# Local value products in four matmuls, earlier in the step, with head split and evacuation reordered

## The chip, the cores and the metric

One core of a Trainium2 chip runs the whole kernel. The metric is device time in microseconds (us) of one execution, here the median of three runs. The engines are TensorE (PE, matmuls; its weight loads are listed apart as PEld), VectorE (DVE), ScalarE (ACT), GpSimd (POOL, almost unused) and SyncE (SP, which issues the DMAs). Each engine runs its own queue of instructions; semaphores tie them together. [...]

## What is computed

```python
# attention: 8 batches x 8 heads, 512 local and 32 global positions, head size 64
k_all = concat([k_g, k_l]);  v_all = concat([v_g, v_l])
out_g = sm(scale * q_g @ k_all.T) @ v_all            # global rows see everything
s_ll  = where(abs(pos[:, None] - pos[None, :]) <= 32, scale * q_l @ k_l.T, -1e9)
s_lg  = scale * q_l @ k_g.T
out_l = sm(concat([s_lg, s_ll])) @ concat([v_g, v_l])   # local rows: a band and the 32 global keys
attn  = concat([out_g, out_l])
# MLP on 4608 tokens of width 512, hidden width 2048
x   = attn.transpose(0, 2, 1, 3).reshape(-1, 512)
h   = maximum(x @ w_in, 0)
out = (h * h) @ w_out
```

## The kernel before

The work is one loop over steps t (from line 593), and three stages run in it side by side. Each step takes one "head", a half sequence (256 rows) of one batch and head; there are 128 of them (NT). In step t the scores and the softmax belong to head t, the transposes and value products to head t-1, and the MLP to step m = t - 9, which is an eighth of the hidden width for a block of 256 rows. So 128 head steps and 136 MLP steps overlap in most of the loop.

Precision is kept by splitting: a value is rounded to a matmul type (`hi`, `ph`, `x_h`, `gh`: the head) and the rounding error is kept in a second tensor (`lo`, `pl`, `x_l`, `gl`: the rest). A product of two split tensors is then three matmuls: head by head, head by rest and rest by head. Heads are made by ACT copies, rests by DVE subtractions. The first 16 heads (`plain`, t < 16) skip this. "Late" below means steps t from 17 to 128, in which head t-1 is not plain.

A late step issues, in this order (line 598 on; each engine keeps its own part of this order, as `InOrder` asks from t = 17):

- `transposes(t-1)`: four PE transposes of the probabilities into the PSUM tile `pt`; `scores(t)`: four matmuls into `s`.
- `gemm1(m, 0)`: 12 matmuls of 256 columns, the first half of the first MLP product, into `h`.
- `pt_split(t-1)`: four ACT copies make the heads `ph` (128x256, 64x128, twice 32x256).
- `softmax1(t)`: DVE, two masked maxima (the profile's CUSTOM_DVE_ANT_0) and their scaling; `softmax2(t)`: ACT, two exponentials. `pt_rest(t-1)`: DVE, three subtractions, into `pl` and the lower half of `ph`.
- Jobs of the global rows at "place 3", and every eighth step `evac` (ACT copies an output block and SP stores it).
- `gemm1(m, 1)`: 12 matmuls. `av(t-1)`: nine value products into the PSUM tile `xa`. `g_scores(t)`: one matmul into `gs`.
- `softmax3(t)`: DVE, sum plus epsilon, reciprocal, and the scaling of both halves of the probabilities.
- `act1(m)`: ACT relu of `h`, then the square, on ACT where t modulo 16 is in `SQ` (2, 3, 4, 5, 14, 15), else a DVE product.
- `x_evac(t-1)`: ACT copies `xa` to `x_h`, DVE subtracts into `x_l`. `split_head(t+1)`: one ACT copy of 864 columns into `hi`, three DVE rests (`lo` 128x448, then parts of `hi`, 64x352 and 32x64).
- `g_evac` in odd steps; jobs at "place 2"; `gemm2(m-1, 0)` and `gemm2(m-1, 1)`: 12 matmuls of 512 columns into `o`; `act2(m)`: ACT copy `gh`, DVE rest `gl`; jobs at "place 1".

The global rows need extra jobs, two groups of heads in 16 steps (line 652). With t modulo 16 they are: `g_soft` (a DVE maximum) in 12 and 2; `g_norm` (DVE) in 13 and 3, and at the end of these steps `g_tr` (four PE transposes into `gt`); `g_rest` and `g_split_v` (ACT and DVE) in 14 and 4, with `g_av` (13 PE matmuls into `gxo`) at the end; `g_x` (four DVE transposes) in 15 and 5 and again in 2 and 8; a second `g_split_v` in 0 and 6, at place 2, and a second `g_av` at the end of 1 and 7.

[...] 

```python
xa = ps_a.tile([64, HALF], F32, tag="xa", name=f"xa{t}")     # av
gt = ps_a.tile([P, 512], F32, tag="xa", name=f"gt{t}")       # g_tr
xo = ps_a.tile([64, P], F32, tag="xa", name=f"gxo{t}_{pair}")  # g_av
```

[...]

Of the kernel before, what the change touches and what calls it, by code (L numbers as in the profile page):

```python
# [7 lines left out]
F32 = mybir.dt.float32  # L8
F32R = mybir.dt.float32r
# [7 lines left out]
P = 128  # L17
HALF = 256
NGR = 2 * B
NT = NGR * H  # L20
QC, KC, VC = HALF, 352, 256
PK = QC + KC + VC
# [4 lines left out]
LAG = 9  # L27
NPLAIN = 16
# [1 line left out]
PLAN = [",,,b", "b,,,b", "b,,,b", "b,,b,", "b,,b,", "b,,b,", "b,,b,", "b,b,,b", "b,b,,b", "bb,bb,bb,bb", "bb,bb,bb,bb", "bbs,bb,bbs,bbs", "bbs,bbs,bbs,bbs", "bbs,bbs,bbs,bbs", "bbs,bbs,bs,s", "ss,s,s,s", "ss,s,s,s", "s,,s,", "s,,s,", "s,,s,", "s,,s,", "s,,s,", "s,,s,"]  # L30
FREE = (17, 17, 17)
LOOK = 2
SQ = (2, 3, 4, 5, 14, 15)
MUL = 9
WCH = 32

# [1 line left out]
def f(ap):  # L38
    return ap.bitcast(F32)
# [19 lines left out]
def attention_moe(  # L59
# [22 lines left out]
    def plain(t):  # L82
        return t < NPLAIN
# [3 lines left out]
    def w_take(n):  # L87
        w_bufs["free"] -= n
# [36 lines left out]
    def split_head(t):  # L125

        hd = heads[t]
        raw = hd["raw"]
        if plain(t):
            return  # L130
        hi = p2.tile([P, PK], F32R, tag="hi", name=f"hi{t}")
        lo = p2.tile([P, QC + 192], F32R, tag="lo", name=f"lo{t}")
        ac.copy(hi, raw)
        ve.tensor_sub(lo, raw[:, KC : KC + QC + 192], f(hi[:, KC : KC + QC + 192]))
        ve.tensor_sub(hi[64:, :KC], raw[64:, :KC], f(hi[64:, :KC]))
        ve.tensor_sub(hi[32:64, PK - 64 :], raw[32:64, PK - 64 :], f(hi[32:64, PK - 64 :]))
        hd["hi"], hd["lo"] = hi, lo

    def scores(t):
# [45 lines left out]
    def softmax3(t):  # L185
        st = heads[t]["st"]
        pr = prob[t % 2]
        ve.tensor_scalar(out=st[:, 6:8], in0=st[:, 4:6], scalar1=1e-9, scalar2=None, op0=ALU.add)
        ve.reciprocal(out=st[:, 0:2], in_=st[:, 6:8])
        for u in range(2):  # L190
            w_ = pr[:, WIN * u : WIN * (u + 1)]
            if MUL <= t < NPLAIN:
                ac.activation(out=w_, in_=w_, func=AF.Copy, scale=st[:, u : u + 1])
            else:
                ve.tensor_scalar(out=w_, in0=w_, scalar1=st[:, u : u + 1], scalar2=None, op0=ALU.mult)
# [6 lines left out]
    def pt_split(t):  # L202
        hd = heads[t]
        if plain(t):
            pts = p2.tile([P, 512], F32, tag="gh", name=f"pts{t}")
            ac.copy(pts, pt)
            hd["pts"] = pts
            return
        ph = p1.tile([P, 640], F32R, tag="ph", name=f"ph{t}")
        pl = p1.tile([P, 256], F32R, tag="pl", name=f"pl{t}")  # L210
        ac.copy(ph[:, :256], pt[:, :256])
        ac.copy(ph[:64, 256:384], pt[:64, 320:448])
        for r in (0, 32):
            ac.copy(ph[r : r + 32, 384:640], pt[64:96, 256:512])
        hd["ph"], hd["pl"] = ph, pl

    def pt_rest(t):
        if plain(t):
            return
        ph, pl = heads[t]["ph"], heads[t]["pl"]  # L220
        ve.tensor_sub(pl, pt[:, :256], f(ph[:, :256]))
        ve.tensor_sub(ph[64:, 256:384], pt[:64, 320:448], f(ph[:64, 256:384]))

        ve.tensor_sub(ph[64:, 384:640], pt[64:, 256:512], f(ph[:64, 384:640]))

    def av(t):
        hd = heads[t]
        c = QC + KC
        if plain(t):

            xa = ps_a.tile([P, HALF], F32, tag="xa", name=f"xa{t}")
            v, pts = hd["raw"][:, c:], hd["pts"]
            mm = [
                (xa, v[:, 0:128], pts[:, 256:512]),
                (xa[:, 0:128], v[:, 64:192], pts[:, 0:128]),
                (xa[:, 128:256], v[:, 128:256], pts[:, 128:256]),
            ]
        else:
            xa = ps_a.tile([64, HALF], F32, tag="xa", name=f"xa{t}")
            vh, vl, ph, pl = hd["hi"][:, c:], hd["lo"][:, QC:], hd["ph"], hd["pl"]  # L240
            mm = []
            for u in range(2):
                o, vs, ps = xa[:, 128 * u : 128 * u + 128], slice(64 * u, 64 * u + 64), slice(128 * u, 128 * u + 128)
                mm += [(o, vh[:, vs], ph[:, ps]), (o, vl[:, vs], ph[:, ps]), (o, vh[:, vs], pl[:, ps])]
            o = xa[:, 64:192]
            mm += [(o, vh[:, 128:192], ph[:, 256:384]), (o, vl[:, 128:192], ph[:, 256:384])]
            mm.append((xa, vh[:, 192:256], ph[:, 384:640]))
        for i, (o, a, b) in enumerate(mm):
            pe.matmul(o, a, b, start=i == 0, stop=i == len(mm) - 1, skip_group_check=True)
        hd["xa"] = xa[:64, :]  # L250

    def x_evac(t):
        g, h = divmod(t, 8)
        xa = heads[t]["xa"]
        r = slice((h % 2) * 64, (h % 2) * 64 + 64)
        if g == 0:
            ac.copy(xg[r, h // 2, :], xa)
        else:
            ac.copy(x_h[r, g % 2, h // 2, :], xa)
            ve.tensor_sub(x_l[r, g % 2, h // 2, :], xa, f(x_h[r, g % 2, h // 2, :]))  # L260
        heads[t] = None

    state = {}
# [176 lines left out]

    moe = {}

    def gemm1(m, j):
        blk, st = divmod(m, 8)
        if j == 0:
            moe["hp"] = ps_h.tile([P, 2, HALF], F32, tag="h", name=f"h{m}")
        hp = moe["hp"]
        if blk == 0:
            mm = [(win(wf, st, j, c), xg[:, c, :]) for c in range(4)]
        else:  # L450
            xh, xl = x_h[:, blk % 2], x_l[:, blk % 2]
            mm = []
            for c in range(4):
                wh, wl = win(whi, st, j, c), win(wlo, st, j, c)
                mm += [(wh, xh[:, c, :]), (wh, xl[:, c, :]), (wl, xh[:, c, :])]
        for n, (a, b) in enumerate(mm):
            pe.matmul(hp[:, j, :], a, b, start=n == 0, stop=n == len(mm) - 1)

    def act1(m):
        hp = moe["hp"]  # L460
        pool, tag = (p2, "gl") if m < 8 else (p1, "r")
        r = pool.tile([P, 2, HALF], F32, tag=tag, name=f"r{m}")
        ac.activation(out=r, in_=hp, func=AF.Relu)
        if m < 8 or m + LAG < NT + 8 and (m + LAG) % 16 in SQ:
            ac.activation(out=r, in_=r, func=AF.Square)
        else:
            ve.tensor_mul(r, hp, r)
        moe["r"] = r
# [33 lines left out]

    def evac(blk, tiles=(0, 1)):
        for i in tiles:
            pool, tag = ((p1, "ot"), (p2, "gl"))[i]
            ot = pool.tile([P, DM], F32, tag=tag, name=f"ot{blk}_{i}")
            ac.copy(ot, moe["o"][i])
            if blk < NGR:
# [80 lines left out]
    for t in range(NSTEP + LAG + 1):  # L589
# [31 lines left out]
        w_tick(t, 0)  # L621
        if live and early:
            g_scores(t)
        if run:
            gemm1(m, 1)
        if prev:
            av(t - 1)
        if live and not early:
            g_scores(t)
        if early and t + 1 < NPLAIN:  # L630
            scores(t + 1)
        if live and not early:
            softmax3(t)
        if run:
            act1(m)
        if prev:
            x_evac(t - 1)
            if plain(t - 1):
                w_take(-1)
        if early:  # L640
            softmax3(t)
        w_tick(t, 1)
        if t + 1 < NT:
            split_head(t + 1)
        if live:
            if t % 2 == 1:
# [124 lines left out]
```

## Time and profile before

| | |
|---|---|
| median of 3 runs | 1068.78 us (1068.65 to 1068.86) |
| the profiled execution | 1068.82 us, its span 1067.0 us |
| PE busy | 1050.4 us, 98% |
| DVE busy | 856.3 us, 80% |
| ACT busy | 753.1 us, 71% |
| DMA | 96.78 MB, mean 91 GB/s |

The span runs from the first to the last profiled instruction; the execution's own time has some 1.8 us more around it. Nearly every instruction is issued through the helper at line 52, so lines do not tell groups apart; the tile names do. A group reads "output<-inputs", then sizes as partitions x elements. A row of the timeline has start, length, engine, line, operation, tiles, shape and count, and in brackets the idle time before it with what ended it. PE rows overlap, because matmuls are pipelined: the distance of two starts is the price of one, not its length.

### The profile page before, as it was taken

To read this page: it belongs to the slowest core of one execution; us is meant where nothing else is said; L and a number is where in the kernel's file an instruction comes from. 1 tells how busy PE (TensorE), PEld (TensorE's weight loads), DVE (VectorE), ACT (ScalarE), POOL (GpSimd) and SP (SyncE) were. 2 spreads that over 40 slices of the span, in tenths; PEclk is the share of its full clock that TensorE was granted. 3 is DMA by queue.
4 is the path that set the end of the run, shared out by engine and by line. 5 is a ranking of instruction groups with operands and counts; after the bars stand their busy time and mean duration, and the time that the engine had idled before them with its cause. 6 is when DMAs were issued, how large, how long until landed. Compare 5 with 4: busy or idle time off the path is not lost.

```text
span 1067.0 us, 21142 instructions
## 1 busy us (share of the span) xinstructions
PE 1050.4 (98%) x7568; PEld 941.7 (88%) x7568; DVE 856.3 (80%) x2687; ACT 753.1 (71%) x1901; POOL 3.9 (0%) x14
## 2 busy tenths in 40 slices
PE   7999999999999999999999999999999999999998
PEld 6776889999998989998999989999999989999896
DVE  5698988898888989988888888888888888874321
ACT  5898877778777776778777777777777787774322
POOL 1000000000000000000000000000000000000000
PEclk9999999999999999999999999999999999999999
DMA  9772132223222322222322222223221322201000
GB/s 372 310 263 74 57 106 76 71 80 98 68 89 64 103 65 83 74 91 77 94 71 82 86 72 76 90 66 100 78 89 55 94 86 66 88 29 33 13 20 20
DMA packets 54312, 96.78 MB, mean 91 GB/s; under 512 B 4288, under 2 KB 29376, under 8 KB 54208
## 3 DMA queue, kind: packets, MB, share of 16 engines
q1 hardware_dynamic: 54064, 95.37, 27.2%
q8 instruction: 60, 0.98, 0.4%
q14 instruction: 44, 0.36, 0.1%
q10 hardware_dynamic: 144, 0.07, 0.0%
HBM read 86.51 MB, written 8.91 MB: 89 GB/s over the span
## 4 chain that ended last, share of the span: by engine, by line
PE 87%; ACT 7%; DVE 4%; issue 1%; DMA 0%; ACTq 0%
PE o L52 33%; PE h L52 32%; PE xa L52 7%; PE s L52 6%; PE pt L52 5%; PE gxo L52 2%; PE gs L52 2%; ACT prob L52 1%; DVE prob L52 1%; ACT r L52 1%; ACT ph L52 1%; ACT hi L52 1%; ACT ot L52 1%; PE gt L52 1%; ACT sg L52 0%
## 5 line engine op out<-in xcount | busy, mean ns | idle before, releaser
L52 PE MATMUL h<-x_h,ws 128*128 128x256 f32 x2048 | 388.9, 283 | 0.0
L52 PEld LDWEIGHTS h<-x_h,ws 128*128 128x128 f32 x2048 | 327.0, 191 | 0.5
L52 PE MATMUL o<-ws,gh 128*128 128x512 f32 x1024 | 321.3, 395 | 0.0
L52 PE MATMUL h<-x_l,ws 128*128 128x256 f32 x1024 | 289.1, 282 | 0.1
L52 PEld LDWEIGHTS o<-ws,gh 128*128 128x128 f32 x1024 | 185.5, 188 | 34.6
L52 PE MATMUL o<-ws,gl 128*128 128x512 f32 x512 | 202.6, 396 | 0.0
L52 PEld LDWEIGHTS h<-x_l,ws 128*128 128x128 f32 x1024 | 195.9, 191 | 0.9 <-DVE x_l L52 0.4
L52 ACT CAST ph<-pt 128x256 fp32r<-128x256 f32 x448 | 141.1, 341 | 67.7 <-PE pt L52 60.8
L52 ACT ACTIVATE prob<-prob,st 128x224 f32<-128x224 f32 x270 | 127.8, 475 | 61.2 <-DVE st L52 59.1
L52 ACT ACTIVATE r<-h 128x512 f32<-128x512 f32 x136 | 81.4, 599 | 112.3 <-PE h L52 112.3
L52 PEld LDWEIGHTS o<-ws,gl 128*128 128x128 f32 x512 | 96.2, 188 | 22.7
L52 DVE CUSTOM_DVE_ANT_0 prob<-s,con 128x224 f32<-128x224 f32 x256 | 90.0, 386 | 24.5 <-PE s L52 23.2
L52 DVE TENSOR_TENSOR gl<-r,gh 128x512 fp32r<-128x512 f32 x128 | 87.9, 686 | 23.3 <-ACT gh L52 20.5
L52 ACT CAST hi<-raw 128x864 fp32r<-128x864 f32 x112 | 102.5, 915 | 1.4
L52 DVE TENSOR_TENSOR r<-h,r 128x512 f32<-128x512 f32 x82 | 56.7, 692 | 51.9 <-ACT r L52 50.6
L52 PE MATMUL xa<-ph,hi 128*64 128x128 f32 x448 | 87.3, 238 | 1.6 <-DVE ph L52 1.2
L52 DVE TENSOR_TENSOR hi<-raw,hi 64x352 fp32r<-64x352 f32 x224 | 82.5, 368 | 6.4
L52 ACT CAST gh<-r 128x512 fp32r<-128x512 f32 x128 | 79.1, 618 | 9.1 <-DVE r L52 8.7
L52 DVE TENSOR_TENSOR ph<-pt,ph 64x128 fp32r<-64x128 f32 x224 | 79.6, 355 | 7.0
L52 DVE TENSOR_TENSOR lo<-raw,hi 128x448 fp32r<-128x448 f32 x112 | 69.6, 622 | 15.3 <-ACT hi L52 12.5
L52 PE MATMUL pt<-con,prob 128*128 128x128 f32 (+1 forms) x512 | 78.2, 274 | 0.7 <-ACT prob L52 0.5
L52 DVE TENSOR_SCALAR prob<-prob,st 128x224 f32<-128x224 f32 x242 | 70.7, 334 | 4.1
(80 smaller groups left out, 1572.7 us busy)
## 6 DMA issues: line engine op xcount, KB each, us to landing
raw<-in_pk_dram SPq DMA_DIRECT2D x127, 432.0 KB, 3.2
wr<-in_w_dram SPq DMA_DIRECT2D x32, 512.0 KB, 7.9
gv<-in_vg_dram SPq DMA_DIRECT2D x32, 320.0 KB, 3.3
out_dram<-ot SPq DMA_DIRECT2D x32, 256.0 KB, 2.2
qr<-in_qg_dram SPq DMA_DIRECT2D x31, 64.0 KB, 2.8
out_dram<-ot SPq DMA_DIRECT2D x8, 64.0 KB, 1.7
con<-in_consts_dram SPq DMA_DIRECT2D x2, 224.0 KB, 5.1
raw<-in_pk_dram SPq DMA_DIRECT2D x1, 304.0 KB, 3.2
```

The source lines that it names most:

```text
L52: r = method(*args, **kwargs)
```

## The change

- The split copy of a head holds value heads and value rests side by side (`vs`, 4 blocks of 64 + 64 columns); the head data differ in one duplicated block that is left out. One ACT copy of 608 columns and one of 4 x 64 replace the one of 864; the DVE rests are 128x256, 64x352 and 128x256.
- The heads and rests of the transposed probabilities lie side by side in one tile `ps`; three ACT copies instead of four, three DVE rests as before.
- `av` has four matmuls (one of 128 columns, three of 256) into `xa`, which is now 128 partitions by 512 columns: rests times heads and heads times rests land in separate parts.
- `x_evac` adds these parts: one ACT copy, then three DVE operations of 64x256 with a new tile `xr`, instead of one.
- `av` stands after the first six matmuls of `gemm1(m, 1)`, not after all twelve.
- The order after `softmax3` is `split_head(t+1)`, `x_evac(t-1)`, `act1(m)`; it was `act1`, `x_evac`, `split_head`.
- In `softmax3`, the scaling of the second half of the probabilities is on ACT; all squares up to t = 127 are on ACT, later ones on DVE.
- The first output tile of `evac` is staged in the buffer of tag "pth" instead of "ot".

```diff
-SQ = (2, 3, 4, 5, 14, 15)
...
+        c = QC + KC
+        hi = p2.tile([P, c + 2 * VC + QC], F32R, tag="hi", name=f"hi{t}")
+        lo = hi[:, c + 2 * VC :]
+        vr = raw[:, c:].rearrange("p (b n) -> p b n", b=4)
+        vs = hi[:, c : c + 2 * VC].rearrange("p (b n) -> p b n", b=4)
+        ac.copy(hi[:, :c], raw[:, :c])
+        ac.copy(vs[:, :, :64], vr)
+        ve.tensor_sub(lo, raw[:, KC:c], f(hi[:, KC:c]))
         ve.tensor_sub(hi[64:, :KC], raw[64:, :KC], f(hi[64:, :KC]))
+        ve.tensor_sub(vs[:, :, 64:], vr, f(vs[:, :, :64]))
...
-            if MUL <= t < NPLAIN:
+            if MUL <= t < NPLAIN or t >= NPLAIN and u == 1:
                 ac.activation(out=w_, in_=w_, func=AF.Copy, scale=st[:, u : u + 1])
...
+        ps = p1.tile([P, 896], F32R, tag="ph", name=f"ph{t}")
+        pb = ps[:, :512].rearrange("p (u h n) -> p u h n", u=2, h=2)
+        ac.copy(pb[:, :, 0, :], pt[:, :256].rearrange("p (u n) -> p u n", u=2))
+        ac.copy(ps[:64, 512:640], pt[:64, 320:448])
+        ac.copy(ps[:64, 640:], pt[64:, 256:])
...
+        ve.tensor_sub(pb[:, :, 1, :], pt[:, :256].rearrange("p (u n) -> p u n", u=2), f(pb[:, :, 0, :]))
+        ve.tensor_sub(ps[64:, 512:640], pt[:64, 320:448], f(ps[:64, 512:640]))
+        ve.tensor_sub(ps[64:, 640:], pt[64:, 256:], f(ps[:64, 640:]))
...
+            xa = ps_a.tile([P, 512], F32, tag="xa", name=f"xa{t}")
+            xb = xa.rearrange("p (u h n) -> p u h n", u=2, h=2)
+            ps, vs = hd["ps"], [hd["hi"][:, c + 128 * i : c + 128 * i + 128] for i in range(4)]
+            both = bass.AP(xa.tensor, xa.offset + 64, [list(xa.ap[0]), [192, 2], [1, 64]])
+            mm = [(both, vs[2], ps[:, 512:640]), (xb[:, :, 0, :], vs[3], ps[:, 640:])]
+            mm += [(xa[:, 256 * u : 256 * u + 256], vs[u], ps[:, 256 * u : 256 * u + 256]) for u in range(2)]
...
+            ac.copy(x0, xb[:64, :, 0, :])
+            ve.tensor_sub(xr, xb[:64, :, 0, :], f(x0))
+            ve.tensor_add(xr, xb[:64, :, 1, :], xr)
+            ve.tensor_add(x1, xb[64:, :, 0, :], xr)
...
-            pe.matmul(hp[:, j, :], a, b, start=n == 0, stop=n == len(mm) - 1)
+            if half in (None, 2 * n // len(mm)):
+                pe.matmul(hp[:, j, :], a, b, start=n == 0, stop=n == len(mm) - 1)
...
-        if m < 8 or m + LAG < NT + 8 and (m + LAG) % 16 in SQ:
+        if m + LAG < NT:
             ac.activation(out=r, in_=r, func=AF.Square)
...
-            pool, tag = ((p1, "ot"), (p2, "gl"))[i]
+            pool, tag = ((p1, "pth"), (p2, "gl"))[i]
...
+        late = prev and not plain(t - 1)
         if run:
-            gemm1(m, 1)
+            gemm1(m, 1, 0 if late else None)
         if prev:
             av(t - 1)
+        if run and late:
+            gemm1(m, 1, 1)
...
         if live and not early:
             softmax3(t)
+        if late:
+            if t + 1 < NT:
+                split_head(t + 1)
+            x_evac(t - 1)
         if run:
             act1(m)
-        if prev:
+        if prev and not late:
             x_evac(t - 1)
```

More of the change, by code (lines that the diff above doesn't have):

```diff
@@ L130, in split_head @@
             return
[L131 to L134, printed above, removed]
+        c = QC + KC
[6 more added lines that the diff above has]
+        ve.tensor_sub(lo, raw[:, KC:c], f(hi[:, KC:c]))
         ve.tensor_sub(hi[64:, :KC], raw[64:, :KC], f(hi[64:, :KC]))
-        ve.tensor_sub(hi[32:64, PK - 64 :], raw[32:64, PK - 64 :], f(hi[32:64, PK - 64 :]))
+        ve.tensor_sub(vs[:, :, 64:], vr, f(vs[:, :, :64]))
         hd["hi"], hd["lo"] = hi, lo
@@ L208, in pt_split @@
             return
[L209 to L215, printed above, removed]
+        ps = p1.tile([P, 896], F32R, tag="ph", name=f"ph{t}")
[3 more added lines that the diff above has]
+        ac.copy(ps[:64, 640:], pt[64:, 256:])
+        hd["ps"], hd["pb"] = ps, pb
     def pt_rest(t):
@@ L219, in pt_rest @@
             return
[L220 to L224, printed above, removed]
+        ps, pb = heads[t]["ps"], heads[t]["pb"]
+        ve.tensor_sub(pb[:, :, 1, :], pt[:, :256].rearrange("p (u n) -> p u n", u=2), f(pb[:, :, 0, :]))
+        ve.tensor_sub(ps[64:, 512:640], pt[:64, 320:448], f(ps[:64, 512:640]))
+        ve.tensor_sub(ps[64:, 640:], pt[64:, 256:], f(ps[:64, 640:]))
     def av(t):
@@ L238, in av @@
         else:
[L239 to L247, printed above, removed]
+            xa = ps_a.tile([P, 512], F32, tag="xa", name=f"xa{t}")
[4 more added lines that the diff above has]
+            mm += [(xa[:, 256 * u : 256 * u + 256], vs[u], ps[:, 256 * u : 256 * u + 256]) for u in range(2)]
         for i, (o, a, b) in enumerate(mm):
             pe.matmul(o, a, b, start=i == 0, stop=i == len(mm) - 1, skip_group_check=True)
-        hd["xa"] = xa[:64, :]
+        hd["xa"] = xa
     def x_evac(t):
@@ L256, in x_evac @@
         if g == 0:
-            ac.copy(xg[r, h // 2, :], xa)
-        else:
-            ac.copy(x_h[r, g % 2, h // 2, :], xa)
-            ve.tensor_sub(x_l[r, g % 2, h // 2, :], xa, f(x_h[r, g % 2, h // 2, :]))
+            ac.copy(xg[r, h // 2, :], xa[:64, :])
+            heads[t] = None
+            return
+        x0, x1 = x_h[r, g % 2, h // 2, :], x_l[r, g % 2, h // 2, :]
+        if plain(t):
+            ac.copy(x0, xa[:64, :])
+            ve.tensor_sub(x1, xa[:64, :], f(x0))
+        else:
+            xb = xa.rearrange("p (u h n) -> p u h n", u=2, h=2)
+            x0, x1 = [x.rearrange("p (u n) -> p u n", u=2) for x in (x0, x1)]
+            xr = p1.tile([P, 2, P], F32, tag="xr", name=f"xr{t}")[r]
+            ac.copy(x0, xb[:64, :, 0, :])
+            ve.tensor_sub(xr, xb[:64, :, 0, :], f(x0))
+            ve.tensor_add(xr, xb[:64, :, 1, :], xr)
+            ve.tensor_add(x1, xb[64:, :, 0, :], xr)
         heads[t] = None
@@ L441, in attention_moe, with gemm1 @@
     moe = {}
-    def gemm1(m, j):
+    def gemm1(m, j, half=None):
         blk, st = divmod(m, 8)
@@ L633, in attention_moe @@
             softmax3(t)
+        if late:
+            if t + 1 < NT:
+                split_head(t + 1)
+            x_evac(t - 1)
         if run:
             act1(m)
-        if prev:
+        if prev and not late:
             x_evac(t - 1)
-            if plain(t - 1):
-                w_take(-1)
+            w_take(-1)
         if early:
@@ L642, in attention_moe @@
         w_tick(t, 1)
-        if t + 1 < NT:
+        if t + 1 < NT and not late:
             split_head(t + 1)
@@ L729 @@
             pk[:, hf, :, 64 * dup : 64 * dup + 64, c + 128 : c + 192] = vw[:, :, 128:192]
-        for dup in range(3):
-            pk[:, hf, :, 32 * dup : 32 * dup + 32, c + 192 : c + 256] = v_g
+        for dup in range(2):
+            pk[:, hf, :, 64 * dup : 64 * dup + 32, c + 192 : c + 256] = v_g
     pk = pk.reshape(NT, P, PK)
```

## The prediction

> **What bounds the kernel now.** I read the page first, then the windows, the chain that ended last, and the timeline of VectorE (DVE), ScalarE (ACT) and TensorE (PE) over single steps; a step is one pass of the main loop. The page says that PE is busy for nearly the whole span.
>
> ```profile
> span 1067.0 us, 21142 instructions
> PE 1050.4 (98%) x7568; PEld 941.7 (88%) x7568; DVE 856.3 (80%) x2687; ACT 753.1 (71%) x1901; POOL 3.9 (0%) x14
> ```
>
> In the steps that the change touches, DVE is nearly as full. The windows give for 150 us: PE 149.63 busy, then PEld, DVE 130.91, ACT 110.59, and a granted clock of 1.00.
>
> ```profile
> 550.00:700.00 150.00, 149.63 (x1127) 136.71 (x1126) 130.91 (x414) 110.59 (x287) 0.00 (x0) 1.00 0.26 82
> ```
>
> The chain that ended last, in a step without jobs, is PE alone (start, length, what):
>
> ```profile
> 588.54 0.14 PE gs L52
> 588.68 2.80 PE o L52 x12
> 591.47 0.44 PE pt L52 x4
> 591.91 0.49 PE s L52 x4
> 592.40 2.88 PE h L52 x24
> 595.28 0.59 PE xa L52 x9
> ```
>
> One such turn is 0.14 + 2.80 + 0.44 + 0.49 + 2.88 + 0.59 = 7.34 us. A first-product matmul of 256 columns costs 2.88/24 = 0.12, and the nine value products 0.59. The late steps (t = 17 to 128) are 112, seven periods of 16. A period is the distance of two global softmax reductions with the same place in it:
>
> ```profile
> 563.62 0.72 DVE L52 TENSOR_REDUCE gst<-sg 128x1 f32<-128x544 f32 x1
> ...
> 685.91 0.72 DVE L52 TENSOR_REDUCE gst<-sg 128x1 f32<-128x544 f32 x1
> ```
>
> That is 122.29 us. Everything below is a new sum for this period; seven times the difference is added to this execution's own 1068.82 us (span 1067.0 and 1.8 around it), which is within 0.04 of the median of the runs.
>
> **The change, part by part.** *Value products.* Nine matmuls of 6x128 + 2x128 + 256 = 1280 columns become four of 128 + 3x256 = 896. At 0.12 for 256 columns that is 0.42 instead of 0.59 to 0.60: 0.18 us less per step on PE, 20 us over 112 steps if PE stays the bound. The strided 128-column one has no row; it lies between 0.06 and 0.12, and I take 0.06, the contiguous price.
>
> *Where they stand.* They move ahead of six first-product matmuls, 0.72 us earlier, and all wait for DVE's rests. From the first masked maximum of a head (call its start W) to the end of the last rest, and on to the end of the reciprocal:
>
> ```profile
> 593.18 0.39 DVE L52 CUSTOM_DVE_ANT_0 prob<-s,con 128x224 f32<-128x224 f32 x1
> ...
> 594.45 0.74 DVE L52 TENSOR_TENSOR ph<-pt,ph 64x128 fp32r<-64x128 f32 x2
> ...
> 595.42 0.17 DVE L52 RECIPROCAL st<-st 128x2 f32<-128x2 f32 x1
> ```
>
> The rests end at W + 2.01, the reciprocal at W + 2.41. The rests keep count and shapes. The second new product needs the last rest, and PE sees such an end 0.15 later (579.94 to 580.09):
>
> ```profile
> 579.20 0.74 DVE L52 TENSOR_TENSOR ph<-pt,ph 64x128 fp32r<-64x128 f32 x2
> ...
> 580.09 0.30 PE L52 MATMUL xa<-ph,hi 128*64 128x256 f32 x1 [0.15 <-DVE ph L52]
> ```
>
> From W + 2.16 PE still has to do 0.36 of value products, 0.72, 0.14 and 2.80, then the transposes (0.44) and scores (0.49), with their filling about 1.1 until the next W, an estimate: 7.3 us. So even a step with nothing else to do gains nothing: this loop is 7.3, against 7.34 now. What is queued behind the wait is the rest of the first product and the whole second product.
>
> *DVE's chain from W to the next W.* New: the second half of the scaling goes to ACT, behind DVE's reciprocal; the split of the next head stands behind it on ACT; DVE's `lo` waits for that split. Rows:
>
> ```profile
> 61.30 0.85 ACT L52 ACTIVATE prob<-prob,st 128x224 f32<-128x224 f32 x2 [0.68 <-DVE st L52]
> ```
> ```profile
> L52 ACT CAST hi<-raw 128x864 fp32r<-128x864 f32 x112 | 102.5, 915 | 1.4
> ...
> L52 ACT CAST ph<-pt 32x256 fp32r<-32x256 f32 x224 | 82.0, 366 | 4.1
> ...
> L52 ACT CAST gh<-r 128x512 fp32r<-128x512 f32 x128 | 79.1, 618 | 9.1 <-DVE r L52 8.7
> L52 DVE TENSOR_SCALAR prob<-prob,st 128x224 f32<-128x224 f32 x242 | 70.7, 334 | 4.1
> ...
> L52 DVE TENSOR_TENSOR hi<-raw,hi 64x352 fp32r<-64x352 f32 x112 | 58.5, 522 | 3.2
> L52 DVE TENSOR_TENSOR r<-h,r 128x512 f32<-128x512 f32 x82 | 56.7, 692 | 51.9 <-ACT r L52 50.6
> ...
> L52 DVE TENSOR_TENSOR x_l<-xa,x_h 64x256 fp32r<-64x256 f32 x120 | 49.6, 414 | 14.8 <-ACT x_h L52 12.9
> ...
> L52 DVE TENSOR_TENSOR pl<-pt,ph 128x256 fp32r<-128x256 f32 x112 | 47.1, 421 | 2.8 <-ACT ph L52 1.9
> ...
> L52 ACT ACTIVATE r<-r 128x512 f32<-128x512 f32 x54 | 34.1, 632 | 1.6
> ```
>
> ACT's scaling: two take 0.85, so one holds ACT for 0.38 and starts 0.04 behind the reciprocal. The split's copy of 608 columns lies between 0.618 (512) and 0.915 (864); on their line 0.70. `lo` starts 0.03 later, at W + 2.41 + 0.04 + 0.38 + 0.70 + 0.03 = W + 3.56. If DVE scaled one half only and did not wait, it would be there at W + 2.41 + 0.04 + 0.33 + 0.03 = 2.81. So DVE stands idle 0.75 us a step. The trace shows that wait, in one step:
>
> ```profile
> 590.40 0.63 DVE L52 TENSOR_TENSOR lo<-raw,hi 128x448 fp32r<-128x448 f32 x1 [0.40 <-ACT hi L52]
> ```
>
> During those 0.40 us nothing behind `lo` on DVE ran. [...]
>
> Then come `lo` 0.42, the 64x352 rest 0.52, the value rest 0.42, each with 0.03 behind it: W + 5.01. The evacuation is now three 64x256 operations of 0.414, not one: end at W + 6.31. Bounds for one of them, strided and from PSUM: 0.37 to 0.45, that is 0.2 either way per step, 22 us in all. Next `gl`, which holds DVE for 0.61 before the next W:
>
> ```profile
> 584.51 0.69 DVE L52 TENSOR_TENSOR gl<-r,gh 128x512 fp32r<-128x512 f32 x1
> 585.12 0.38 DVE L52 CUSTOM_DVE_ANT_0 prob<-s,con 128x224 f32<-128x224 f32 x1
> ```
>
> W + 6.31 + 0.03 + 0.61 = 6.95. The squares leave DVE in ten steps of sixteen (0.69 each) and are not in this chain; ACT hides them: from W + 3.53 it has two copies of 256 columns (about 0.37 each, as the 32x256 one), relu and square (0.63 each) and `gh` 0.62, done at 6.15, before `gl` at 6.34. Without these 0.2 us of cover `gl` would wait for ACT. ACT's three copies of the transposed probabilities instead of four (0.366 for the fourth) help only where a step says so below.
>
> [...] With both halves on DVE (0.58 in this trace) `lo` would start at W + 3.05, half a microsecond earlier in every step that DVE leads, some 50 us in all.
>
> *The jobs.* They stand in DVE's queue between the rests and the reciprocal, or ahead of `gl`, and now add in full:
>
> ```profile
> 570.73 0.27 DVE L52 COPY sg<-sg 128x32 f32<-128x32 f32 x2
> ...
> 571.47 0.17 DVE L52 TENSOR_SCALAR st<-st 128x2 f32<-128x2 f32 x1
> ...
> 577.93 0.39 DVE L52 CUSTOM_DVE_ANT_0 prob<-s,con 128x224 f32<-128x224 f32 x1
> ...
> 580.57 0.69 DVE L52 TENSOR_TENSOR gvl<-gv,gvh 128x512 fp32r<-128x512 f32 x1 [0.62 <-ACT gvh L52]
> ...
> 581.59 0.17 DVE L52 TENSOR_SCALAR st<-st 128x2 f32<-128x2 f32 x1
> ...
> 582.60 0.42 DVE L52 TENSOR_TENSOR x_l<-xa,x_h 64x256 fp32r<-64x256 f32 x1
> ...
> 587.16 0.85 DVE L52 STREAM_TRANSPOSE xg<-gxs 32x32 f32<-32x32 f32 x4
> ...
> 591.86 0.48 DVE L52 TENSOR_TENSOR sg<-gs,sg 64x160 f32<-64x160 f32 x2
> ```
>
> `g_evac` in odd steps 0.5; `g_soft` 0.72 + 0.03 (its reduction is above); `g_norm` 571.47 - 570.73 = 0.74; `g_x` 0.88; `g_split_v` 581.59 - 580.57 = 1.02, and in the steps where it stands early the softmax begins at W + 3.66 instead of 2.04, 1.62 later.
>
> *The tile xa.* The global transposes and products use the same PSUM buffer as the value products, and wait until DVE has read it:
>
> ```profile
> 583.07 0.13 PEld L52 LDWEIGHTS gxo<-gvh,pth 128*64 128x64 f32 x1 [0.18 <-DVE x_l L52]
> ```
>
> From the end of `x_l` (583.02) to the next W (585.12) are 2.10. That end moves back by the two added operations and the wait. Where the transposes follow, another chain runs to the next W:
>
> ```profile
> 697.34 0.45 PE gt L52 x4
> ...
> 700.22 0.39 DVE prob L52
> ```
>
> 2.43 from their end, less the fourth copy's 0.37: 2.06; with their 0.45, the 0.05 until weights are loaded (583.02 to 583.07) and about 0.25 of loading and filling, an estimate, W is 2.81 after the evacuation.
>
> *The sum of a period*, by t modulo 16. 10: the loop, 7.3. 9 and 11: 6.95 + 0.5 = 7.45 each. 12: 7.70. 8: 7.83. 0 and 6: 7.97 each. 2 (`g_x` and `g_soft`): 8.58. 5 and 15: 8.33 each. 1 and 7 (global products): 6.31 + 2.10 = 8.41 each. 13 and 3 (`g_norm`, then transposes): 6.31 + 0.74 + 2.81 = 9.86 each. 14 and 4: 6.31 + 1.62 + 2.10 = 10.03 each. Together 135.5, or 13.2 more than now. Seven periods: 92.5 us; 1068.8 + 92.5 = 1161, said as 1160.
>
> *Costed at nothing*: the head's data (same size, same DMAs); output staging in another buffer, which the global transposes fill only in steps 13 and 3 and the staging uses in 2 and 10; `raw`, which is freed earlier and never later; the steps before 17 and after 128, whose PE work is the same.
>
> **The rivals.** *PE stays the bound.* If DVE and ACT found room, only the 0.18 would show: 1068.8 - 20.2 = 1048.6, faster. For it: DVE's busy time is 131 of 150 now, and added and removed DVE work nearly cancel (0.83 more for the evacuation; 0.25 less by the scaling in place of two, and 0.69 less in ten of sixteen). The place is DVE's wait at `lo` and the price 0.18 a step; it decides once DVE's period, 135.5 in my sum, falls below 122.3 - 16 x 0.18 = 119.4, for which 0.75 a step and the waits at xa must both go. Against it: ACT and DVE run in order, and no step offers DVE other work at that place.
>
> *DVE leads, but xa is free in time.* Then 1 and 7 cost 7.45 each, 14 and 4 6.95 + 1.62 = 8.57, and 13 and 3 7.45 + 0.74 and about 1.0 for the transposes' rests, an estimate: 129.3 a period, 7.0 more than now, and 1118 in the end. For it: the wait at xa is 0.18 in the row above. Against: DVE's chain reaches xa about 2 us later in 14 and 4.
>
> *A wait for a wait.* Only the loop of 7.3 matters, and the job steps stay as they are: 1066 to 1072, no change.
>
> **How the numbers follow.** My forecast 0.63, DVE alone 0.20, PE bound 0.12, no change 0.05. Within 0.2% (2.1 us, about what a measurement of this kernel can tell from no change) I put 0.04, and the last 0.01 with faster: faster 0.13, same 0.04, slower 0.83. The range takes in the forecast with its unknown prices (22 us for the evacuation, 8 for the split's copy) and the second rival with the same below it, 1090 to 1190; it leaves out 0.17.
>
> **What would show it.** Right: about 0.75 us of idle time before each `lo`, released by ACT; PE idle before the second value product, and 1 to 2 us before the global products in steps 14 and 4, released by `x_l`; a period near 135. Wrong: DVE idle before the masked maximum, released by PE, in most steps, and a PE without gaps.

## The result, and the profile after

The new kernel takes 1175.87 us (median of 4 runs, 1174.46 to 1176.15), the old one beside it 1068.72 (4 runs, 1068.55 to 1068.86): 1.0999 times as long, with a 95% interval of 1.0983 to 1.1016. The forecast was 1160 in a range of 1090 to 1190. The profiled execution took 1175.79 with a span of 1173.8.

The page of the new kernel, its span and busy line, and the engine shares of the chain that ended last:

```profile
span 1173.8 us, 20253 instructions
PE 1074.0 (91%) x7008; PEld 936.6 (80%) x7008; DVE 884.8 (75%) x2734; ACT 813.1 (69%) x2078; POOL 3.9 (0%) x14
DVE 44%; PE 32%; ACT 16%; issue 7%; DMA 0%; ACTq 0%; DVEq 0%
```

PE issues 560 matmuls fewer (five in each of 112 steps), yet it has no work in 9% of the span. No engine is full now: PE 91%, DVE 75%, ACT 69%. So no single engine is the bound. The chain passes from one to the other, and DVE holds the largest share of it, 44%. The windows say the same for 150 us, where DVE was at 130.91 before and is at 119.87 now:

```profile
550.00:700.00 150.00, 134.77 (x920) 119.10 (x921) 119.87 (x372) 107.63 (x281) 0.00 (x0) 1.00 0.24 74
```

One late step on DVE's timeline (start, length, operation, in brackets the idle time before it and who ended it). It is step 12 by t modulo 16:

```profile
620.58 0.72 DVE L51 TENSOR_REDUCE gst<-sg 128x1 f32<-128x544 f32 x1
...
621.60 0.17 DVE L51 RECIPROCAL st<-st 128x2 f32<-128x2 f32 x1
621.80 0.34 DVE L51 TENSOR_SCALAR prob<-prob,st 128x224 f32<-128x224 f32 x1
622.97 1.42 DVE L51 TENSOR_TENSOR hi<-raw,hi 128x256 fp32r<-128x256 f32 x3 [0.83 <-ACT hi L51]
624.42 0.42 DVE L51 TENSOR_TENSOR xr<-xa,x_h 64x256 f32<-64x256 f32 x1
624.87 0.42 DVE L51 TENSOR_TENSOR xr<-xa,xr 64x256 f32<-64x256 f32 x1
625.32 0.43 DVE L51 TENSOR_TENSOR x_l<-xa,xr 64x256 fp32r<-64x256 f32 x1
625.76 0.69 DVE L51 TENSOR_TENSOR gl<-r,gh 128x512 fp32r<-128x512 f32 x1
626.47 0.39 DVE L51 CUSTOM_DVE_ANT_0 prob<-s,con 128x224 f32<-128x224 f32 x1
```

(`lo` now lies inside the tile `hi`, so its row carries that name; the three rests of the head are the x3.) After the reciprocal DVE scales one half, then stands idle for 0.83 until ACT has copied the next head, then runs through to the next masked maximum with no gap. ACT's timeline of the same place shows what DVE waited for: ACT itself waited for the reciprocal, scaled the other half, and only then began the split's two copies.

```profile
621.86 0.48 ACT L51 ACTIVATE prob<-prob,st 128x224 f32<-128x224 f32 x1 [1.32 <-DVE st L51]
622.25 0.99 ACT L51 CAST hi<-raw 128x608 fp32r<-128x608 f32 x2
```

The groups of the whole execution (busy time and mean, then the idle time before, with its releaser):

```profile
L51 DVE TENSOR_TENSOR hi<-raw,hi 128x256 fp32r<-128x256 f32 x224 | 95.3, 425 | 97.9 <-ACT hi L51 94.5
...
L51 PE MATMUL xa<-ph,hi 128*128 128x256 f32 x336 | 66.5, 306 | 12.7 <-DVE ph L51 12.2
...
L51 PE MATMUL gxo<-gvh,pth 128*64 128x128 f32 x160 | 31.2, 228 | 28.3 <-DVE x_l L51 26.6
L51 PE MATMUL xa<-ph,hi 128*128 128x128 f32 x112 | 30.7, 274 | 34.3 <-DVE ph L51 34.3
```

94.5 us before the head's rests, released by ACT, is 0.84 a step. PE's idle time lies near the places that were foreseen: 26.6 before the global products (1.78 to 1.80 a time in steps 14 and 4 from step 30 on, where 1 to 2 was said), and 46.5 before the value products. There the prediction named the second one; the larger part, 34.3, stands before the first, which waits for DVE's rests as well, and 12.2 before the others.

A period of 16 steps, between the same two global reductions as before:

```profile
620.58 0.72 DVE L51 TENSOR_REDUCE gst<-sg 128x1 f32<-128x544 f32 x1
...
757.85 0.72 DVE L51 TENSOR_REDUCE gst<-sg 128x1 f32<-128x544 f32 x1
```

It is 137.27 us instead of 122.29, 14.98 more; seven periods make 104.9 of the 106.8 by which the spans differ. The remaining 2 us belong to steps 17 to 32, which are 17.1 us longer than before and not 15.0. Steps 19 and 20 hold the excess, and there the granted clock fell twice for a few microseconds (0.66 in this window around the first fall, in the column after the busy times). That the lower clock is the cause is likely, but no run shows it apart.

```profile
130.00:135.00 5.00, 4.37 (x17) 3.86 (x18) 3.90 (x15) 3.63 (x11) 0.00 (x0) 0.66 0.00 0
```

### The profile page after: what moved, and what is told of

Same layout as the page of the kernel before. It is cut to its first block, busy times and chain, and to the rows that moved or that the text cites. A ratio compares the mean times of both kernels' runs of the same rounds, so it can differ in the third digit from the quotient of the medians.

```text
span 1173.8 us, 20253 instructions
## 1 busy us (share of the span) xinstructions
PE 1074.0 (91%) x7008; PEld 936.6 (80%) x7008; DVE 884.8 (75%) x2734; ACT 813.1 (69%) x2078; POOL 3.9 (0%) x14
## 4 chain that ended last, share of the span: by engine, by line
DVE 44%; PE 32%; ACT 16%; issue 7%; DMA 0%; ACTq 0%; DVEq 0%
PE o L51 11%; PE h L51 10%; DVE hi L51 9%; DVE prob L51 6%; DVE ph L51 6%; DVE xr L51 6%; ACT hi L51 6%; ACT prob L51 4%; DVE gl L51 4%; DVE st L51 4%; PE xa L51 3%; PE gxo L51 3%; PE s L51 2%; PE pt L51 2%; DVE x_l L51 2%
## 5 line engine op out<-in xcount | busy, mean ns | idle before, releaser
L51 PE MATMUL h<-x_h,ws 128*128 128x256 f32 x2048 | 407.1, 283 | 0.0
L51 ACT ACTIVATE prob<-prob,st 128x224 f32<-128x224 f32 x382 | 181.9, 478 | 208.3 <-DVE st L51 208.1
L51 DVE TENSOR_TENSOR hi<-raw,hi 128x256 fp32r<-128x256 f32 x336 | 153.8, 458 | 99.4 <-ACT hi L51 94.5
L51 PE MATMUL xa<-ph,hi 128*128 128x128 f32 x448 | 96.0, 298 | 46.9 <-DVE ph L51 46.5
L51 DVE TENSOR_TENSOR ph<-pt,ph 128x256 fp32r<-128x256 f32 x336 | 126.5, 376 | 5.6 <-ACT ph L51 0.6
L51 PEld LDWEIGHTS xa<-ph,hi 128*128 128x128 f32 x448 | 67.6, 188 | 70.7 <-issue 38.1
L51 ACT CAST hi<-raw 128x608 fp32r<-128x608 f32 x224 | 111.2, 544 | 0.0
L51 ACT CAST ph<-pt 128x256 fp32r<-128x256 f32 x336 | 100.3, 333 | 14.0 <-PE pt L51 7.4
L51 ACT ACTIVATE r<-r 128x512 f32<-128x512 f32 x119 | 75.1, 631 | 3.6
L51 PE MATMUL s<-hi 128*128 128x224 f32 x448 | 77.2, 294 | 0.2 <-DVE hi L51 0.2
```

Source lines behind the costliest of these rows:

```text
L51: r = method(*args, **kwargs)
```

## The experiments

The theory: DVE's chain from one masked maximum to the next sets the time. Three pieces lengthened it at once: the wait of `lo` for an ACT copy that stands behind ACT's scaling, two added evacuation operations, and, in some steps, the late release of `xa` to the global work. Rivals: the value products' new place ahead of six matmuls makes PE wait and is the cause itself; or the steps are set by PE and ACT so that taking DVE's pieces away gives little. The kernels come in groups; each group names the one it starts from. All ratios are to the old kernel on the same chip.

**One part at a time, from the new kernel.** First, both halves scaled on DVE again:

```diff
-            if MUL <= t < NPLAIN or t >= NPLAIN and u == 1:
+            if MUL <= t < NPLAIN:
```

> The changed kernel with both halves of the probabilities scaled on VectorE again; all else as changed. My theory (VectorE's own chain sets the pace, and the scaling on ScalarE, which stands ahead of the head split there, makes VectorE idle before the lo rest): lo starts 3.05 us after the first masked maximum W instead of 3.59, the 0.83 us of idle time before it goes, and nearly every step is half a microsecond shorter although VectorE has 0.25 us more work: 7 to 8 us less per period of 16, 1118 to 1128 us in all. Rival (the early value products make TensorE wait, and nothing else matters): VectorE gets 0.25 us a step more to do ahead of the next head, so no gain, 1176 to 1204 us.

1126.76 us, ratio 1.0545 (1.0527 to 1.0562): 49 us less than the new kernel, and the part of the theory on the scaling holds, although the time lies at the slow end. The groups show why the wait did not go altogether:

```profile
L51 DVE TENSOR_TENSOR hi<-raw,hi 128x256 fp32r<-128x256 f32 x224 | 94.8, 423 | 28.0 <-ACT hi L51 24.6
L51 ACT CAST hi<-raw 128x608 fp32r<-128x608 f32 x112 | 78.7, 702 | 65.4 <-PE xa L51 65.4
```

ACT is now early, and its copy waits for PE: the tile `hi` has two buffers, and the one that the copy takes is still read by the value products. A second wait stood behind the first. On DVE it appears only where a step has no job that delays the reciprocal (0.49 in steps 0, 1, 6, 7, 9 and 11, 0.71 in step 10).

Second, the value products behind all twelve matmuls, as before the change:

```diff
-            gemm1(m, 1, 0 if late else None)
+            gemm1(m, 1)
 ...
-        if run and late:
-            gemm1(m, 1, 1)
```

> The changed kernel with the value products after all twelve matmuls of the first product's second half. My theory: TensorE's waits before the second value product (46.5 us in the page's row) go, but VectorE leads, so the time stays within 6 us of 1176 us; the idle time turns up before the scores or at the tile xa. Rival (the early placement is the cost): the 46.5 us come back, about 1128 us.

1189.69, ratio 1.1128 (1.1103 to 1.1154). The rival falls: the early place is not what costs. The theory missed too, since the time rose by 14 and was to stay within 6. The steps have the same length as in the new kernel, except where the clock fell behind a long PE pause. PE's timeline and the windows:

```profile
648.50 0.24 PE L51 MATMUL gxo<-gvh,pth 128*64 128x128 f32 x1 [2.49 <-DVE x_l L51]
...
650.91 0.44 PE L51 MATMUL h<-x_h,ws 128*128 128x256 f32 x1
651.15 0.41 PE L51 MATMUL h<-x_l,ws 128*128 128x256 f32 x1
...
653.69 0.28 PE L51 MATMUL h<-x_l,ws 128*128 128x256 f32 x1
```
```profile
646.50:650.00 3.50, 1.50 (x18) 1.50 (x18) 2.42 (x6) 1.97 (x4) 0.00 (x0) 0.92 0.35 127
650.00:653.50 3.50, 3.50 (x21) 3.50 (x20) 2.23 (x10) 1.94 (x7) 0.00 (x0) 0.60 0.00 0
```

PE stood still for 2.49 us, then ran at 0.24 a matmul (650.91 to 651.15) instead of 0.12 until about 653, when the clock came back (1.00 from 653.50 to 660). The mean granted clock of this execution, which took 1186.12 us, is 0.985; that of the new kernel's profiled one is 0.996. The new kernel has two such stretches, in steps 19 and 20; later the same pause is 1.78 there, because the six matmuls left for after the value products fill 0.7 of it, and the clock stays up (1.00 from 152 to 1057). So the early place is worth 14 us here.

Third, the evacuation ahead of the split:

```diff
         if late:
+            x_evac(t - 1)
             if t + 1 < NT:
                 split_head(t + 1)
-            x_evac(t - 1)
```

> The changed kernel with the evacuation of xa before the split of the next head on ScalarE and VectorE. My theory (the evacuation comes too late, the shared tile xa then stops TensorE, and VectorE idles before lo): the evacuation fills part of the idle time (lo no longer waits 0.83 us; a shorter wait of about 0.4 us stands before the evacuation), its end moves from W + 6.37 to about W + 4.6, so the global products and transposes no longer wait for it: a third of a microsecond less in the ten plain steps of a period, about 1 us less in the two with transposes and 1.7 us less in the two with split and products, 9 us a period, about 1111 us. Rival (only the sum of VectorE's work counts, 75% busy or not): the sum is the same, so 1170 to 1180 us.

1128.83, ratio 1.056 (1.0544 to 1.0576): 47 us less, and 18 above the number expected. `xa` is free earlier (idle time before the global products 0.7 instead of 26.6) and `lo` finds its operand ready; but the evacuation now waits for ACT in nearly the same way, 74.5 us in all:

```profile
L51 DVE TENSOR_TENSOR xr<-xa,x_h 64x256 f32<-64x256 f32 x112 | 46.8, 418 | 74.5 <-ACT x_h L51 74.5
L51 PE MATMUL gxo<-gvh,pth 128*64 128x128 f32 x160 | 30.9, 227 | 2.5 <-DVE x_l L51 0.7
```

Fourth, without the two added operations, so that the products with a rest are left out of `x_l`:

```diff
-            ve.tensor_sub(xr, xb[:64, :, 0, :], f(x0))
-            ve.tensor_add(xr, xb[:64, :, 1, :], xr)
-            ve.tensor_add(x1, xb[64:, :, 0, :], xr)
+            ve.tensor_sub(x1, xb[:64, :, 0, :], f(x0))
```

> The changed kernel without the two added VectorE operations of the evacuation: the products with a rest are computed but left out of x_l. My theory (the three operations lie on VectorE's chain and in front of the release of xa): 0.89 us less in the steps that VectorE or xa leads, down to TensorE's own loop of about 7.3 us in the plain steps: 10 to 11 us less per period, about 1101 us. Rival (the wait for ScalarE sets the pace and the evacuation runs in its shadow): no change, 1170 to 1180 us.

1131.18, ratio 1.0583 (1.0568 to 1.0599): 45 us less where 75 were expected. The two operations cost 0.9 a step on DVE, 100 us in 112 steps; more than half of that is not regained, because DVE then waits for ACT elsewhere: `gl` for `gh` (25.3 us between 300 and 1010; the 0.2 us of cover that ACT had behind DVE, named in the prediction, is used up) and the evacuation of the global scores for ACT's `sg` (18.7). The three parts taken singly give 49 + 47 + 45 = 141, more than the 107 that the change costs in all. Taken off the new kernel, 141 would leave 1035, below the 1048.6 that the prediction gives to a PE that never waits; so by that sum their prices can't add. No run takes all three away at once.

**Two evacuation operations instead of three, and both halves scaled on DVE.** The first version gives up a part of the four-matmul layout: the products of head and rest for the two own blocks are separate, six matmuls that add up the rests in PSUM.

```diff
-            mm += [(xa[:, 256 * u : 256 * u + 256], vs[u], ps[:, 256 * u : 256 * u + 256]) for u in range(2)]
+            for u in range(2):
+                o = xa[:, 128 * u : 128 * u + 128]
+                mm += [(o, vs[u], ps[:, 256 * u : 256 * u + 128]), (o[:64], vs[u][:, :64], ps[:, 256 * u + 128 : 256 * u + 256])]
 ...
-            ve.tensor_sub(xr, xb[:64, :, 0, :], f(x0))
-            ve.tensor_add(xr, xb[:64, :, 1, :], xr)
-            ve.tensor_add(x1, xb[64:, :, 0, :], xr)
+            ve.tensor_sub(xr, xa[:64, :], f(x0))
+            ve.tensor_add(x1, xa[64:, :], xr)
```

> The changed kernel with both halves scaled on VectorE, and with the local value products laid out otherwise: head rows and rest rows of v times the head of the probabilities (128 columns), then v's head times the rest of the probabilities added to the same columns by TensorE. The columns streamed stay 896, in six matmuls; xa has 256 columns, and the evacuation needs two VectorE operations instead of three. My theory (VectorE's chain up to the release of xa): 0.45 us less than with the scaling change alone in the two steps with split and products, and less in the others, which come to the loop of 7.3 us: 127 to 129 us per period, 1100 to 1113 us. Rival (the layout matters only by TensorE's work): as the scaling change alone, 1127 us, or more for two more weight loads.

1113.9, ratio 1.0424 (1.0408 to 1.0439), 0.9 above the range expected. Then the same with the evacuation first:

> The kernel of two operations and scaling on VectorE, early value products, and the evacuation of xa ahead of the head split. My theory: xa is free before TensorE comes to the global products, so these steps fall to about 8.1 us and those with transposes to about 9.2; the plain steps stay at the loop of 7.3: 126 to 127 us per period, 1095 to 1105 us.

1102.6, ratio 1.0318 (1.03 to 1.0335), inside its range. And the first one with the value products behind all twelve matmuls:

> The kernel of two operations and scaling on VectorE, with the value products after all twelve first-product matmuls. My theory: VectorE's chain is now below TensorE's step in the plain steps, so here the place matters: the loop of 7.3 us becomes TensorE's own 7.1 us and small delays are absorbed; the steps with split and products still wait for xa. 10 to 40 us less than with the early place: 1065 to 1100 us. Rival (the early place frees xa sooner and is needed for that): slower than the early place.

1107.45, ratio 1.0365 (1.0348 to 1.0382), 7 above the range expected. Once DVE's chain is shorter, the old place is the better one, by 6.5 us; it was the worse one by 14 as long as PE paused. What remains is again ACT's copy into `hi`, waiting for the value products (99.0 us before it). From here, the evacuation was put ahead of the split only in the four steps whose end or whose follower needs `xa` for global work:

```diff
+            if t % 16 in (3, 4, 13, 14):
+                x_evac(t - 1)
             if t + 1 < NT:
                 split_head(t + 1)
-            x_evac(t - 1)
+            if t % 16 not in (3, 4, 13, 14):
+                x_evac(t - 1)
```

> The kernel of two operations, scaling on VectorE and late value products, with the evacuation ahead of the split only in steps 3, 4, 13 and 14 of 16, where jobs hold VectorE back and xa is filled long before. My theory: nothing but short waits is left: TensorE's work per period is 117.6 us by the rows (16 x 0.18 less than now), VectorE's about 118.5, so about 121 us per period and 1050 to 1072 us, at or below the kernel before. Rival (any order with the compact products loses, since VectorE has one more operation per step): above 1075 us.

1084.49, ratio 1.0148 (1.0133 to 1.0163): above the range expected by 12, since the wait for `hi` stayed:

```profile
L51 DVE TENSOR_TENSOR hi<-raw,hi 128x256 fp32r<-128x256 f32 x224 | 94.9, 424 | 45.7 <-ACT hi L51 41.8
L51 ACT CAST hi<-raw 128x608 fp32r<-128x608 f32 x112 | 78.5, 701 | 80.3 <-PE xa L51 79.8
```

That wait was then taken away at its source. The value heads and rests get a tile of their own, so that the copy of keys and queries no longer depends on the value products:

```diff
-        hi = p2.tile([P, c + 2 * VC + QC], F32R, tag="hi", name=f"hi{t}")
-        lo = hi[:, c + 2 * VC :]
+        hi = p2.tile([P, c + QC], F32R, tag="hi", name=f"hi{t}")
+        lo = hi[:, c:]
+        vt = p2.tile([P, 2 * VC], F32R, tag="vt", name=f"vt{t}")
```

> The mixed-order kernel with the value heads and rests in a tile of their own (two buffers) instead of behind the keys in hi. Only this differs. Theory from the traces: the split's first copy on ScalarE waited for the value products of head t-1 (62 us released by the value products in the row of ScalarE's waits), because head t+1 takes the buffer of head t-1; with the values apart, that copy waits for nothing, lo starts about 3.1 us after W instead of 3.65 to 3.93 in the plain steps, and seven to nine steps a period are 0.2 to 0.6 us shorter: 121 to 122.5 us a period, 1058 to 1070 us, about the kernel before or a little below. Rival (the wait is that for the value copy, the second one, which overwrites what the products free): no change, 1080 to 1087 us.

1068.84, ratio 1.0001 (0.9992 to 1.0011): the time of the kernel before. The rival of the run before, that any order loses because VectorE has one operation more per step, is answered too: that operation is still there, and nothing is lost. The 16 us that were left beside the kernel with one tile are the price of the shared buffer. The groups show the wait moved to the small value copy, which nothing urgent follows:

```profile
L51 ACT CAST hi<-raw 128x608 fp32r<-128x608 f32 x112 | 77.5, 692 | 0.3
...
L51 ACT CAST vt<-raw 128x256 fp32r<-128x256 f32 x112 | 45.5, 407 | 47.5 <-PE xa L51 47.5
```

**ACT's scaling: its price or its place?** The two kernels here have the change's four matmuls and three operations, with the late value products, the mixed order and the own tile of the kernel above. They differ in one thing. In one, ACT scales where the change put it; in the other, the same ACT instruction (`scale_late`) stands behind `split_head` and `x_evac`:

```diff
+            if t >= NPLAIN and u == 1:
+                continue
 ...
+        if live and not early:
+            scale_late(t)
```

> The new kernel's four matmuls and three-operation evacuation, with the value products behind all twelve matmuls, the evacuation ahead of the split in steps 3, 4, 13 and 14 only, the value operand in a tile of its own, and ScalarE's scaling of the second half issued behind the split's copies and the copy of the evacuation. If the price of that scaling is its place in ScalarE's queue ahead of the split, lo finds its operand ready, VectorE's chain comes to some 117 us a period, and the loop of PE (0.4 of value products in place of 0.6, first-product matmuls unchanged) to about the same: a period of 120 to 121, so 1055 to 1062. If the dearer evacuation (0.83 more on VectorE) is a price of its own that no order hides, the time is 1072 or more.

> The same kernel with the scaling in the place where the change put it, ahead of the split's copies on ScalarE. If its place is the price, the idle time of about 0.8 before lo is back in every step, released by ScalarE, the period is 6 to 10 us longer than that of the kernel beside it, and the time 1105 to 1130. If the place is nothing once the value operand has its own tile, both kernels come out within 10 us of one another.

Behind the copies: 1075.86, ratio 1.0068 (1.0055 to 1.0081). Ahead of them: 1144.98, ratio 1.0714 (1.0698 to 1.0731). The place of one ACT instruction of under half a microsecond is worth 69 us, or 9.9 a period, at the upper end of the 6 to 10 that were expected; both times lie some 15 us above their ranges. With it ahead, DVE's 0.83 is back in the steps without a changed order:

```profile
L51 DVE TENSOR_TENSOR hi<-raw,hi 128x256 fp32r<-128x256 f32 x112 | 47.4, 423 | 72.0 <-ACT hi L51 71.6
```

With it behind, 7.1 us are left before that group. But 1075.86 isn't the 1055 to 1062 that was expected for this case: it stays 7 above the kernel before. The expectation would read that as a price of the dearer evacuation; the last kernel below speaks against it. A plain stretch shows that PE saves what the four products can save: the chain that ended last is PE alone, with turns of 7.14 us.

```profile
673.96 2.87 PE h L51 x24
676.83 0.47 PE xa L51 x4
677.30 0.13 PE gs L51
677.43 2.79 PE o L51 x12
680.22 0.44 PE pt L51 x4
680.66 0.44 PE s L51 x4
681.10 2.87 PE h L51 x24
```

Four products take 0.47, against 0.59 for nine. The period is nonetheless 122.96 in the median of its steps, because steps 0, 2, 4, 6, 14 and 15 take 7.6 to 8.0. There DVE, at 133.38 busy of 150 us (130.91 before), goes through jobs, evacuation and `gl` up to the next maximum with no gap in steps 2 and 15, and with one of 0.5 to 0.8 for ACT's `gvh` in the others.

```profile
550.00:700.00 150.00, 148.31 (x1037) 134.52 (x1036) 133.38 (x426) 121.40 (x322) 0.00 (x0) 1.00 0.25 80
```

**A last try for a faster kernel**: the version at 1068.84 with its second scaling on ACT behind the copies, the same edit as above.

> The kernel with six value products, a two-operation evacuation and a value tile of its own, which came out at 1068.84, with ScalarE's scaling of the second half behind the split's copies instead of on VectorE. VectorE gets 0.33 a step back, ScalarE takes 0.4 to 0.48 more, PE does the same. If VectorE's queue is what still lengthens the steps with jobs, their excess of about 4 a period over the plain steps' 7.25 shrinks by a third to a half: a period of 120 to 121 and 1055 to 1063. If ScalarE's queue or PE sets those steps, the time stays within 3 of 1069 or goes above.

1079.04, ratio 1.0096 (1.0082 to 1.011), 10 us slower than with both halves on DVE. DVE's load fell (124.24 of 150 us busy, from 130.40), but the steps with jobs now wait for ACT: steps 3 and 13 go from 8.76 and 8.84 to 9.34 and 9.22, where the evacuation of the global scores waits for ACT's copy.

```profile
DVE sg L51 <- ACT sg L51: 28.7, 42, 1.0
DVE gvl L51 <- ACT gvh L51: 18.7, 20, 1.3
```

In the version with both on DVE the same two waits are 9.2 and 15.1 (between 300 and 950 us).

This kernel also differs from the one at 1075.86 in the layout alone: six products and two evacuation operations here, four and three there. It is the slower one by 3.2 us, although its DVE has 9 us less to do in 150 (124.24 against 133.38). Steps 2, 4 and 14 do take 0.25 to 0.43 more with three operations, but the other steps give that back and more. So once ACT's scaling stands behind the copies, the dearer evacuation is no price on balance, and the 7 us above the kernel before aren't explained by it. The likelier cause is the scaling on ACT, which costs 10 here; the change's layout with a value tile of its own and both halves scaled on DVE would tell, and was not run. No version tried beats the kernel before.

## Why the prediction was right

Direction, mechanism and size hold: 1160 forecast, 1175.87 measured, 92.5 of the 107.1 us. The range, 1090 to 1190, was wide enough to hold a rival as well (1118), so it is the steps below that bear the mechanism out. W is again the start of a head's first masked maximum. Point by point:

**DVE's chain in a step without jobs.** `lo` was to start at W + 3.56 behind 0.75 of idle time; it starts at W + 3.59 behind 0.83. The evacuation was to end at W + 6.31 and ends at W + 6.37. The three operations, which no row showed before, cost 0.42, 0.42 and 0.43 against 0.414 taken: the 22 us kept for them in the range were not needed. The 0.75 was short by 0.08 from both ends: DVE was free 0.05 earlier, and ACT handed over 0.03 later.

**Nothing fills the wait.** The prediction took this from one row, with 0.40 of idle time in which nothing behind `lo` ran. The gap is there in step after step (94.5 us in 112), and with the one ACT instruction moved out of the way 69 us came back in the pair of kernels that differ in nothing else. That part is shown.

**The steps one by one** (medians of t modulo 16, from one masked maximum to the next):

| step | forecast | measured | before |
|---|---|---|---|
| 10 | 7.3 | 7.58 | 7.27 |
| 9, 11 | 7.45 | 7.39, 7.71 | 7.26, 7.47 |
| 12, 8 | 7.70, 7.83 | 7.91, 7.99 | 7.11, 7.30 |
| 0, 6 | 7.97 | 8.13, 8.10 | 7.31, 7.60 |
| 2 | 8.58 | 8.78 | 7.68 |
| 5, 15 | 8.33 | 8.24, 8.59 | 7.71, 8.06 |
| 1, 7 | 8.41 | 8.42 | 7.29, 7.36 |
| 13, 3 | 9.86 | 9.95 | 9.23 |
| 14, 4 | 10.03 | 10.05 | 7.20 |

The sum is 137.3 for 135.5. The steps with global work, where the new chain through `xa` was built from rows of two different places, are within 0.1; steps 14 and 4 alone give 5.7 of the 15 a period. The error sits in the others: eight steps are 0.13 to 0.28 longer than forecast, and steps 9 and 5 are 0.06 and 0.09 shorter. It has four sources. The evacuation ends 0.06 later. `gl` holds DVE for 0.71 in even steps (625.76 to 626.47 above), where the one row that the sum used gave 0.61. Steps 11 and 15 have one more DVE operation that `g_evac` at 0.5 had left out:

```profile
479.96 0.48 DVE L51 TENSOR_TENSOR sg<-gs,sg 64x160 f32<-64x160 f32 x2
480.47 0.29 DVE L51 TENSOR_TENSOR qgz<-qr,qgz 128x128 fp32r<-128x128 f32 x1
```

And in step 10 ACT copies an output block between the exponentials and the scaling, so that the wait before `lo` is 1.32 there and not 0.83, and DVE sets this step, not the loop of 7.3. DVE's row first, then ACT's:

```profile
470.07 1.42 DVE L51 TENSOR_TENSOR hi<-raw,hi 128x256 fp32r<-128x256 f32 x3 [1.32 <-ACT hi L51]
```
```profile
468.00 1.07 ACT L51 COPY ot<-o 128x512 f32<-128x512 f32 x2
468.96 0.49 ACT L51 ACTIVATE prob<-prob,st 128x224 f32<-128x224 f32 x1
469.34 1.01 ACT L51 CAST hi<-raw 128x608 fp32r<-128x608 f32 x2
```

So of the 14.6 us between the forecast and what came, 7 x 1.8 = 12 are these terms, and 2 lie in steps 19 and 20, where the clock fell; the prediction had not thought of that.

**The value products.** They were priced at 0.42, the strided one of 128 columns at 0.06, the low end of 0.06 to 0.12. The chain above gives 0.47 for the four, 0.05 more. In the one place of the new kernel where they run without a wait, they start at 153.57, 153.63 and 153.80, and what follows them at 154.04. So 0.06 fits the strided one; the excess stands behind the second product (0.17 to the third start, where 0.12 was taken), and the last two take 0.24. The 0.12 by which 0.47 is under the old 0.59 would be 13 us instead of 20 if PE were the bound. It made no difference in the new kernel, where PE waits. Its step 10, the only one that the forecast gave to PE's loop of 7.3, is set by DVE, so that term stays untested; with the products in the old place PE's turn is 7.14.

**The scaling on ACT.** The prediction worked out from its rows that scaling on ACT loses some 50 us, and undoing that part alone gave 49. But the pair of kernels that differ in its place shows that most of it is where the instruction stands in ACT's queue: behind the copies it costs 69 less than ahead of them. Behind the copies ACT's scaling still loses 10 us to DVE's (1079.04 against 1068.84). Those 10 aren't the cost of the instruction alone either, since DVE then waits for ACT in other places (`sg` and `gvl` in the rows of that run).

**The rivals.** PE stays the bound: of the kernels with four products, the one at 1075.86 comes nearest to it. It needed another place for the scaling, for the value products and for four of sixteen evacuations, and a second tile; and even then DVE and its waits for ACT in the steps with jobs kept it from the 1048.6 of this rival. DVE leads but `xa` is free in time: 1118 was its number, and with the evacuation first 1128.83 came out. A wait for a wait: no run supports it.

**What the prediction did not see**: the buffer of `hi`, whose release by the value products stands right behind the wait it described. It cost nothing in the new kernel, since ACT was later still (0.0 us of idle time before its copy into `hi`). It decided much of what the repairs were worth, and five expectations (the evacuation first, the operations left out, and the three versions before the own tile that missed or touched their upper end) were too low because of it or of ACT's next operation.

## What to carry to other kernels

When an operation moves to a less busy engine, look at what stands behind it in that engine's queue: here 0.4 us of scaling put ahead of a copy that another engine waits for cost 69 us more than the same instruction behind the copy. Take a wait away and ask what is late next, the buffer included: operands that are released at different times belong in different tiles, since a shared one is held by its slowest reader (16 us here). Fewer matmul columns pay only where the matmul engine sets the step; here they were worth 20 us at best by the forecast, and a longer chain on the engine next in line turned that into a loss of 107. A busier engine need not be the slower kernel: of the two layouts with the same place for the scaling, the one with 9 us more of DVE work in 150 was 3 us faster.

## What the runs showed of the hardware

In the new kernel the granted clock falls twice in the steps from 17 to 128: it is 0.50 over 131.40 to 134.70, behind a PE pause of 1.85 us that ended at 130.47, and 0.50 over 148.50 to 151.80, behind one of 2.37 that ended at 148.16. A matmul of 256 columns takes 0.21 to 0.24 there instead of 0.12. Thirteen pauses of 1.78 to 1.80 in the same execution, which end from 232.77 to 1056.35, brought none: the clock is 1.00 from 152 to 1057. In the new kernel with late value products the pause of 2.49 that ended at 648.50 was followed by a clock of 0.60 over 650.00 to 653.50, again with 0.21 to 0.24 a matmul. What parts the pause of 1.85 from those of 1.80 isn't shown.

The columns that are streamed are not the whole price of a product. The kernel with six value products streams 896 columns like the one with four, and its chain shows 0.53 instead of 0.47:

```profile
664.98 0.53 PE xa L51 x6
665.69 2.79 PE o L51 x12
```

By columns alone both would take 0.42, an estimate at 0.12 for 256. Six products load 4 x 128 + 2 x 64 = 640 columns of weights, four load 512, the old nine 576. The wider load took longer: 188 ns in the mean for the 128 columns of a value product of the new kernel, against 135 to 137 for the 64 of one of the kernel before. But the nine have fewer columns of weights than the six and take longer (0.59), so neither count alone gives the times, and what adds 0.05 for the four and 0.11 for the six isn't shown. In the old nine a product of 128 columns takes 0.06 to the next start, as counted; behind the second of the four 0.17 passes and not 0.12. So heads and rests side by side save less than the count of columns says: 0.12 by the two chains (0.59 and 0.47), where the forecast took 0.18.
